# State products of batches 1 to 3 over the whole array, preparation split into single operations, last row pair by seven products, and a new order: a retention layer with an MLP mixer on one core

## The chip, the cores and the metric

The kernel runs on one core of one Trainium2 chip. The metric is device time in microseconds for one execution. Before the change three executions took 189.84 us in the median (189.46 to 190.31). A change of less than 0.5% is about what a measurement of this kernel cannot tell from none.

## The reference, cut to what matters

```python
def _attn_ref(q, k, v):                     # (4, 8, 768, 64) each
    B, H, S, D = q.shape
    gamma = 1.0 - 2.0 ** (-5.0 - np.arange(H))
    scale = 1.0 / np.sqrt(D)
    state = np.zeros((B, H, D, D))
    for t in range(S):
        state = gamma[None, :, None, None] * state + np.einsum('bhd,bhe->bhde', k[:, :, t], v[:, :, t])
        y[:, :, t] = scale * np.einsum('bhd,bhde->bhe', q[:, :, t], state)

def _moe_ref(x, w_tok1, w_tok2, w_ch1, w_ch2):   # x: (4, 768, 512), heads side by side
    xt = x.transpose(0, 2, 1)
    h = np.maximum(xt @ w_tok1, 0.0) @ w_tok2    # 768 -> 256 -> 768 over the tokens
    u = x + h.transpose(0, 2, 1)
    return u + np.maximum(u @ w_ch1, 0.0) @ w_ch2    # 512 -> 1536 -> 512 over the channels
```

## The kernel before, in words

The 768 time steps of a batch are cut into 6 chunks of 128, and the 8 heads into 4 pairs. `front(b, p)` does batch b and head pair p, 16 in all:

- K and Q are scaled by decay tables (`decayed`, L519 on ACT and L521 on DVE; tables `gk`, `gy`), and turned (`kT`, `qT`): in batch 0 on the PE (L551, L553) with an evacuation by DVE or ACT (L562, L567), in batches 1 to 3 by a DMA transpose of K and Q.
- The state of a chunk is a 64 x 64 product of K and V for each head (L582). Its 5 chunks x 2 heads are ten matmuls on quarter tiles of the array, called "wide" in the code, into one PSUM bank. Five steps on DVE then sum the states up: a copy (L592) and four multiply-adds (L594, tile `U`), each of 128 x 64 with the product read from PSUM. ACT or DVE writes them as `cross` (L605, L607).
- Scores K Q (L623, on half tiles, "high") are masked on DVE (L630, tile `am`) and multiplied by V (L641); the cross terms are added (L651). The result is `x16` (L663).
- The token mixer follows: L676, relu, L696. Its output is cast as `u16` and copied to `X`; `u16` is turned into `uT` (L732 and L738 in batch 0, a DMA in the others).

`back(b)` is the channel mixer of a batch. Batch 0 widens with plain products (L766), the others with seven half products in place of eight (`widen7`, L838, with sums on DVE, L810, kept pieces `us` on ACT or DVE, L791, and joins on DVE, L859). Then `narrow7` makes two row chunks by seven products (L962) of six matmuls of 256 columns, with four sums on DVE (L941) and five additions into `X` (L976). Only the last two chunks of batch 3 go through `narrow` (L909, added by L918): twelve matmuls of 512 columns for the one, and for the other twelve each of 256, 128 and 128 columns.

The order is written out by hand: `ORDERED` lists every operation by its number, two characters each, and `WAYS` says which of its engines does it. `arrange` goes through the list with planned costs (`act`, `dve`, the class `Rings` for the DMA queues, `FREE` for the start of each engine) and assigns buffers and PSUM banks; what is issued on each engine follows that order. Where the plan has the PE idle for over 400 ns in the first 21 us, matmuls of a zero tile into bank 7 are put in (`FILL`, L1079).

The first loads go through SP (two Q tiles called `hs` and a K tile called `us`, in float32); all others through POOL. The preparation ahead of the first products is a few operations: `away` and `since` by iota on POOL, `lgs` (L400) and the `lnh` and `gp` memsets on DVE, the `gq` tables (four Exp on ACT, L425) and `gk`, `gy` (L404, L405).

## Time and profile before

| | us |
|---|---|
| median of three executions | 189.84 |
| the profiled execution's own time | 188.9 |
| its span | 187.1 |
| PE busy | 179.3 |
| DVE busy | 168.0 |
| ACT busy | 122.5 |
| POOL busy | 52.7 |

The span runs from the first instruction of the program to its last; 1.8 us of the execution's own time lie around it. Busy time of the PE counts matmuls until their results are out, so that one overlaps the next: how far apart two matmuls start tells what each costs. The granted TensorE clock was 0.998 in the mean.

### The profile page before, as it was taken

To read this page: it belongs to the slowest core of one execution; us is meant where nothing else is said; L and a number is where in the kernel's file an instruction comes from. 1 tells how busy PE (TensorE), PEld (TensorE's weight loads), DVE (VectorE), ACT (ScalarE), POOL (GpSimd) and SP (SyncE) were. 2 spreads that over 40 slices of the span, in tenths; PEclk is the share of its full clock that TensorE was granted. 3 is DMA by queue.
4 is the path that set the end of the run, shared out by engine and by line. 5 is a ranking of instruction groups with operands and counts; after the bars stand their busy time and mean duration, and the time that the engine had idled before them with its cause. 6 is when DMAs were issued, how large, how long until landed. Compare 5 with 4: busy or idle time off the path is not lost.

```text
span 187.1 us, 5262 instructions
## 1 busy us (share of the span) xinstructions
PE 179.3 (96%) x2103; PEld 136.4 (73%) x2103; DVE 168.0 (90%) x430; ACT 122.5 (65%) x277; POOL 52.7 (28%) x61
## 2 busy tenths in 40 slices
PE   7899999999999999999999999999999999999990
PEld 2465799666788988877668889966679986668960
DVE  5479999998999999999999999998799999888871
ACT  0869789347899999999978785595754126551000
POOL 7994496562644442266004000000000000000000
PEclk9999999999999999999999999999999999999999
DMA  6999999999999999699999997242013054700062
GB/s 160 202 158 193 178 195 195 186 188 204 158 156 150 150 177 141 101 106 152 163 204 128 139 169 162 112 89 41 0 56 46 0 155 182 272 1 4 0 233 106
DMA packets 92249, 25.31 MB, mean 135 GB/s; under 512 B 81984, under 2 KB 89280, under 8 KB 92224
## 3 DMA queue, kind: packets, MB, share of 16 engines
q0 software_dynamic: 67184, 12.78, 88.1%
q1 hardware_dynamic: 23456, 9.64, 24.7%
q10 hardware_dynamic: 1584, 2.56, 3.7%
q8 instruction: 16, 0.26, 0.6%
q14 instruction: 9, 0.07, 0.1%
HBM read 26.74 MB, written 6.29 MB: 177 GB/s over the span
## 4 chain that ended last, share of the span: by engine, by line
PE 81%; DVE 10%; ACT 5%; issue 2%; POOL 1%; POOLq 0%; DVEq 0%; ACTq 0%
PE bank L962 25%; PE bank L838 18%; PE bank L766 9%; PE bank L676 6%; PE bank L696 5%; DVE am L630 3%; PE bank L909 3%; PE bank L641 3%; PE bank L623 2%; PE bank L651 2%; PE bank L582 2%; PE bank L1079 2%; PE bank L551 2%; DVE U L594 1%; ACT cross L605 1%
## 5 line engine op out<-in xcount | busy, mean ns | idle before, releaser
L791 ACT COPY us<-bank 128x384 f32<-128x384 f32 (+1 forms) x43 | 18.5, 438 | 24.4 <-PE bank L962 10.2
L630 DVE TENSOR_TENSOR am<-bank,mask 128x384 f16<-128x384 f32 x64 | 32.7, 547 | 1.0 <-PE bank L623 1.0
L786 ACT ACTIVATE h<-bank 128x384 f16<-128x384 f32 x45 | 21.5, 499 | 10.2 <-PE bank L766 7.2
L962 PEld LDWEIGHTS <-hs 128*128 128x128 f16 x264 | 24.7, 98 | 2.7
L962 PE MATMUL bank<-wsum,hs 128*128 128x256 f16 x198 | 26.4, 273 | 0.0
L482 POOL DMA_DIRECT2D v<-in_v_dram x16 | 16.7, 1042 | 34.2 <-PE bank L651 22.3
L838 PE MATMUL bank<-hs,late 128*128 128x384 f16 x108 | 23.8, 326 | 0.3 <-DVE hs L810 0.2
L859 DVE CUSTOM_DVE_ANT_0 h<-bank,us 128x384 f16<-128x384 f32 x36 | 19.1, 550 | 3.2 <-ACT us L791 1.9
L962 PEld LDWEIGHTS <-h 128*128 128x128 f16 x198 | 18.7, 98 | 2.5
L976 DVE TENSOR_TENSOR X<-X,bank 128x256 f32<-128x256 f32 x44 | 17.8, 414 | 1.5 <-PE bank L962 1.2
L838 PEld LDWEIGHTS <-late 128*128 128x128 f16 x144 | 13.3, 98 | 8.0 <-issue 0.2
L766 PE MATMUL bank<-uT,wc 128*128 128x384 f16 x96 | 17.7, 326 | 0.0
L962 PE MATMUL bank<-wc,h 128*128 128x256 f16 x132 | 17.5, 273 | 0.0
L594 DVE SCALAR_TENSOR_TENSOR U<-U,gp,bank 128x64 f32<-128x64 f32 x64 | 16.6, 274 | 0.5
L482 POOL DMA_DIRECT2D k<-in_k_dram x15 | 15.7, 1045 | 4.2 <-ACT X L663 1.7
L838 PE MATMUL bank<-uT,wc 128*128 128x384 f16 x72 | 16.3, 326 | 0.0
L605 ACT ACTIVATE cross<-U,gp 64x320 f16<-64x320 f32 x27 | 15.1, 558 | 0.7 <-DVE U L594 0.3
L696 PE MATMUL bank<-h,wt 128*128 128x128 f16 x192 | 15.0, 219 | 0.0
L663 ACT CAST x<-bank 128x384 f16<-128x384 f32 x30 | 13.9, 487 | 1.5 <-PE bank L838 0.9
L838 PEld LDWEIGHTS <-wc 128*128 128x128 f16 x108 | 10.1, 98 | 5.2
L676 PE MATMUL bank<-x,wt 128*128 128x128 f16 x192 | 13.3, 219 | 0.3 <-ACT x L663 0.2
L696 PEld LDWEIGHTS <-wt 128*128 128x128 f16 x192 | 12.2, 98 | 1.7
(87 smaller groups left out, 354.9 us busy)
## 6 DMA issues: line engine op xcount, KB each, us to landing
out_dram<-X SPq DMA_DIRECT2D x14, 256.0 KB, 2.8
v<-in_v_dram POOLq DMA_DIRECT2D x16, 192.0 KB, 7.2
k<-in_k_dram POOLq DMA_DIRECT2D x15, 192.0 KB, 7.7
q<-in_q_dram POOLq DMA_DIRECT2D x14, 192.0 KB, 8.0
wc<-in_moe_w_ch_dram POOLq DMA_DIRECT2D x5, 512.0 KB, 13.5
out_dram<-X ACTq DMA_DIRECT2D x9, 256.0 KB, 2.3
hs<-in_q_dram SPq DMA_DIRECT2D x2, 384.0 KB, 5.1
wc<-in_moe_w_ch_dram POOLq DMA_DIRECT2D x2, 256.0 KB, 8.0
```

Of the source, the lines that this page charges most:

```text
L482: (nc.sync if hard else nc.gpsimd).dma_start(out=tile_of(s, [P, 2, NC, D], FP if hard else F16), in_=src.rearrange("h (c p) d -> p (h c) d ...
L594: nc.vector.scalar_tensor_tensor(out=u[:, c], in0=u[:, c - 1], scalar=gp[:, p:p + 1], in1=st, op0=ALU.mult, op1=ALU.add)
L630: nc.vector.tensor_tensor(am, SC[g].tile[:, :m * P].rearrange("p (i t) -> p i t", t=P), mask.to_broadcast([P, m, P]), ALU.mult)
L676: nc.tensor.matmul(acc[:, jt * P:(jt + 1) * P], wt1[:, i, jt * P:(jt + 1) * P], X16.tile[:, i].rearrange("p h d -> p (h d)"), start=(i == ...
L696: nc.tensor.matmul(Y[j].tile[:, 2 * i * D:2 * (i + 1) * D], wt2[:, jt, t], H1.tile[:, jt], start=False, stop=(jt == NJ - 1), skip_group_ch ...
L766: nc.tensor.matmul(acc[:, :SH], wc1[:, ct, ft * P:(ft + 1) * P], UT.tile[:, ct, sh * SH:(sh + 1) * SH], start=(ct == 0), stop=(ct == NP - 1))
L786: nc.scalar.activation(out, src, AF.Relu)
L791: (nc.scalar.copy if e == "ACT" else nc.vector.tensor_copy)(out, src)
L838: nc.tensor.matmul(acc[:, :SH], left(ct), r[:, ct], start=first and ct == 0, stop=ct == C2 - 1, skip_group_check=True)
L859: nc.vector._custom_dve(TENSOR_ADD_SAT, out=h(m, sh), in0=R.tile[:, :SH], in1=KS.tile[:, j], s0=BIG, s1=0.0)
L962: nc.tensor.matmul(acc[:, lo], l[:, j], r[:, j], start=first and j == 0, stop=j == K2 - 1, skip_group_check=True)
L976: nc.vector.tensor_tensor(dst(), dst(), b_(), ALU.add)
```

## The change

The state products of batches 1 to 3 (`FULL`) become five matmuls of 128 x 128 in place of ten on quarter tiles: both heads' K against both heads' V. Four chunks go to one PSUM bank and the fifth to another. Of each 128 x 128 result only the two diagonal 64 x 64 blocks are states. Four copies bring them to `U` in SBUF (two of 64 x 256, two of 64 x 64; each on ACT or DVE by `WAYS`), and the four multiply-adds then work in `U` in place. The copy L592 falls away for these twelve fronts.

The preparation is cut into single operations that the order can place one by one; a tiny Exp (`warm`) stands first on ACT, so that the table load comes there. `LAST7` turns the last two chunks of batch 3 over to `narrow7`. Several dependencies on a buffer's first user are now order alone (`behind`). Planned costs change (`act`, `decayed`, `FREE`, `OPENING`, `SOFT`), and `ORDERED` and `WAYS` are new throughout.

```diff
+    OPENING = 2900
-    SOFT = 0.6
+    SOFT = 0.55
...
-FREE = dict(PE=300, ACT=2500, DVE=900, POOL=900, SP=750)
+FREE = dict(PE=300, ACT=1150, DVE=1090, POOL=1200, SP=750)
...
-    "0a090d0b0c000408030e01050j1e060h071j0f0i021f1g0g1k1h1l1i1m0l1n1P1Q1t1O1o1x1p0k1q2s1w1R1v1T1S1u0m1V1U1r2t0o23"
+    "0o0l00070q020s0p080a090g0x0h011s0v0306040b0c1x220t0d1y270r0m0i0e0u1t1u280f1v1w0w230k1H0n241K250z1I2G261L2H0y"
...
-    LAST7 = False
+    WIDE7 = {0: (), 1: range(6), 2: range(6), 3: range(6)}
+    FULL = (1, 2, 3)
+    SOURCE = ()
+    LAST7 = True
...
+    def emit():
+        nc.scalar.activation(warm, zero[:, :1], AF.Exp)
+    prep("warm", "ACT", 1350, emit)
...
-    def emit():
-        nc.scalar.activation(gk, lgs, AF.Exp, scale=-1.0)
-        nc.scalar.activation(gy, lgs, AF.Exp, bias=lnsc, scale=1.0)
-    g_op = prep("ACT", 380, emit, [lgs_op])
+    gk_op = prep("gk", "ACT", 130, lambda: nc.scalar.activation(gk, lgs, AF.Exp, scale=-1.0), [lgs_op])
+    gy_op = prep("gy", "ACT", 200, lambda: nc.scalar.activation(gy, lgs, AF.Exp, bias=lnsc, scale=1.0), [lgs_op])
...
+        gq_ops.append(prep("gq", "ACT", 605, emit, [since_op, lnh_op, lgm_op], [] if p else [GQ], [SINCE, GQ] if p else [SINCE]))
...
+    cross_ops = [prep("cross", "DVE", 330, lambda t=t: nc.vector.memset(t, 0.0)) for t in cross]
...
+        if b in FULL:
+            STs = [Slot(FA, good=2), Slot(FA)]
+
+            def emit():
+                for st in STs:
+                    tile_of(st, [P, 512], FP)
+                for c in range(NC - 1):
+                    nc.tensor.matmul(STs[c // 4].tile[:, c % 4 * P:(c % 4 + 1) * P], K.tile[:, c].rearrange("p h d -> p (h d)"),
+                                     V.tile[:, :, c], start=(c % 4 == 0), stop=True, skip_group_check=True)
+            pp = op(one("PE", (280, 440), emit), kl + [vl], STs, [K, V], key="st")
+            cp = []
+            for k in range(2):
+                for j in range(2):
+                    def emit(e, k=k, j=j):
+                        u = tile_of(US, [P, NC - 1, D], FP) if US.tile is None else US.tile
+                        n_ = 1 if k else 4
+                        copy(e, u[rows_of(j), 4 * k:4 * k + n_],
+                             STs[k].tile[rows_of(j), :n_ * P].rearrange("p (c x) -> p c x", x=P)[:, :, j * D:(j + 1) * D])
+                    cp.append(op(either(emit, ACT=act(64 if k else 256), DVE=dve(64 if k else 256)), [pp], [] if cp else [US],
+                                 ([US] if cp else []) + [STs[k]], behind=cp[0] if cp else None, key="sd"))
+            for c in range(1, NC - 1):
+                def emit(c=c):
+                    nc.vector.scalar_tensor_tensor(out=US.tile[:, c], in0=US.tile[:, c - 1], scalar=gp[:, p:p + 1],
+                                                   in1=US.tile[:, c], op0=ALU.mult, op1=ALU.add)
+                prev = op(one("DVE", (195, 280), emit), (cp[2:] if c == NC - 2 else cp[:2]) + [gp_ops[p], prev], [], [US], key="u")
```

What the new order puts where is shown at three places.

On SP, the first loads of the program, before (`hs` are the Q tiles of pairs 0 and 1, `us` is the K tile of pair 0; the turns behind them belong to later batches):

```order
L478 DMA hs_85<-in_q_dram 128x2x384
L482 DMA us_92<-in_k_dram 128x12x64
L478 DMA hs_94<-in_q_dram 128x2x384
L540 DMA_TRANSPOSE kT_1352<-k_1219 128x6x128
L540 DMA_TRANSPOSE qT_1444<-q_1430 128x6x128
```

and now:

```order
L487 DMA hs_86<-in_q_dram 128x2x384
L487 DMA hs_92<-in_q_dram 128x2x384
L491 DMA us_105<-in_k_dram 128x12x64
L549 DMA_TRANSPOSE kT_1435<-k_1353 128x6x128
L549 DMA_TRANSPOSE kT_1490<-k_1458 128x6x128
```

The K tile of pair 0 has moved from second to third. On DVE, the work just ahead of the first masked score (`am`), before:

```order
L521 TENSOR_SCALAR k_170<-us_92,gk 128x6x64
L562 TENSOR_TENSOR qT_175<-bank_151,X_125 128x768
L592 COPY U_210<-bank_197 128x64
L594 SCALAR_TENSOR_TENSOR U_210<-U_210,gp,bank_197 128x64
L521 TENSOR_SCALAR k_214<-k_101,gk 128x6x64
L594 SCALAR_TENSOR_TENSOR U_210<-U_210,gp,bank_197 128x64
L630 TENSOR_TENSOR am_239<-bank_223,mask 128x384
```

and now (`X` holds the `gq` tables; `cross`, `gp`, `lnh` and `mask` are preparation):

```order
L571 TENSOR_TENSOR qT_158<-bank_140,X_111 128x768
L449 MEMSET cross_78 128x320
L445 MEMSET gp 64x1
L446 MEMSET gp 64x1
L433 MEMSET lnh 64x1 x2
L530 TENSOR_SCALAR k_182<-us_105,gk 128x6x64
L571 TENSOR_TENSOR qT_185<-bank_160,X_111 128x768
L576 COPY kT_204<-bank_197 128x768
L448 TENSOR_SCALAR mask<-away 128x128
L449 MEMSET cross_79 128x320
L530 TENSOR_SCALAR k_208<-k_103,gk 128x6x64
L665 TENSOR_TENSOR am_232<-bank_216,mask 128x384
```

Two turned Q tiles, the evacuation of `kT` and pieces of the preparation now stand ahead of the first masked score, and the first state sums (`U`) no longer do. On ACT, the first two fronts of batch 1 now have copies of states among the relus of batch 0's channel mixer (`h`):

```order
L377 ACTIVATE h_876<-bank_897 128x384
L382 COPY U_970<-bank_949 64x256
L528 ACTIVATE k_980<-k_739,gk 128x6x64
L382 COPY U_970<-bank_950 64x64
L382 COPY U_992<-bank_973 64x256
L377 ACTIVATE h_874<-bank_926 128x384
L377 ACTIVATE h_874<-bank_988 128x384
L377 ACTIVATE h_874<-bank_983 128x384
L377 ACTIVATE h_874<-bank_967 128x384
L640 ACTIVATE cross_78<-U_970,gp 64x5x64 x2
```

Before, ACT had no such copies: the first sum of a front read the product from its bank on DVE. Of the 48 copies, 31 stand on ACT (16 of 64 x 256, 15 of 64 x 64) and 17 on DVE (8 and 9).

280 lines of the change are left out of this document (159 added, 121 removed).

## The prediction

> **What bounds the kernel now.** First the page: busy shares and the chain that ended last, by engine.
>
> ```profile
> PE 179.3 (96%) x2103; PEld 136.4 (73%) x2103; DVE 168.0 (90%) x430; ACT 122.5 (65%) x277; POOL 52.7 (28%) x61
> ...
> PE 81%; DVE 10%; ACT 5%; issue 2%; POOL 1%; POOLq 0%; DVEq 0%; ACTq 0%
> ```
>
> The PE carries four fifths of the chain. Next the windows by stage (PE, PEld, DVE, ACT, POOL busy) and the PE's waits from 26 to 154 us.
>
> ```profile
> 26.00:94.00 68.00, 67.81 (x887) 52.19 (x884) 65.75 (x162) 57.97 (x133) 31.24 (x32) 1.00 1.96 160
> 94.00:154.00 60.00, 59.77 (x698) 48.44 (x697) 57.17 (x141) 38.04 (x91) 2.03 (x2) 1.00 0.55 98
> 170.00:180.00 10.00, 10.00 (x98) 8.72 (x96) 8.45 (x21) 0.74 (x2) 0.00 (x0) 1.00 0.11 40
> ```
>
> ```profile
> PE bank L838 <- DVE hs L810: 0.2, 1, 0.2
> ```
>
> From 26 us on the PE is busy 127.58 of 128 us, and its longest wait is 0.2 us. DVE is nearly as full, 122.92 of 128, and ACT has 57.97 of 68 up to 94 us. So matmul time saved after 26 us shows in the span, as long as work added to DVE and ACT keeps inside 5.1 and 10 us of idle time. Ahead of 26 us it is otherwise: there the PE runs zero matmuls to fill gaps, and DVE sets the pace.
>
> **The opening.** DVE between 11 and 26 us, and what starts the first product:
>
> ```profile
> 11.00:26.00 15.00, 14.15 (x251) 10.90 (x250) 14.56 (x38) 11.66 (x24) 9.55 (x13) 1.00 1.81 182
> ```
>
> ```profile
> 5.60 2.50 ACT L425 ACTIVATE X<-us,lnsc,lnh 128x384 f32<-128x384 f32 x4
> 8.01 0.19 ACT L404 ACTIVATE gk<-lgs 128x8 f32<-128x8 f32 x1
> ```
>
> ```profile
> 8.23 0.42 DVE L521 TENSOR_SCALAR k<-us,gk 128x384 f16<-128x384 f32 x1 [2.07 <-ACT gk L404]
> ```
>
> ```profile
> 1.77 0.81 SPq L478 DMA_DIRECT2D hs<-in_q_dram  x1
> ```
>
> ```profile
> hs<-in_q_dram SPq DMA_DIRECT2D x1, 384.0 KB, 6.7
> ```
>
> ```profile
> 6.29 3.51 PE L1079 MATMUL bank<-zero 128*128 128x384 f16 x13
> 9.63 0.50 PE L553 MATMUL bank<-ident,k 128*128 128x128 f16 x6
> ...
> 11.02 0.51 PE L623 MATMUL bank<-qT,kT 64*128 64x128 f16 x12
> ```
>
> ```profile
> 26.14 0.65 PE L623 MATMUL bank<-qT,kT 64*128 64x128 f16 x12
> ```
>
> Before, the decay of K waits 2.07 us for `gk`, which stands behind four Exp. The change takes that wait away: `gk` now stands behind one. But the K tile is now third on SP, and the third load landed at 1.77 + 6.7 = 8.5 us, where the decay began at 8.23. So the table is no longer late, the load is, and I book no gain there. After it thirteen zero matmuls hold the PE until the turn of K at 9.63; the new order has nine at that place.
>
> I take the first score no earlier than the 11.02 of before, and count the DVE work from there to the fourth score (26.14). DVE starts its next instruction about 0.08 us before the last one's duration is over: three masks take 1.48, so one costs (1.48 - 0.55) / 2 = 0.465, by these rows.
>
> ```profile
> 12.55 1.48 DVE L630 TENSOR_TENSOR am<-bank,mask 128x384 f16<-128x384 f32 x3
> ```
>
> ```profile
> L562 DVE TENSOR_TENSOR qT<-bank,X 128x768 f16<-128x768 f16 x8 | 7.4, 947 | 0.0
> L567 DVE COPY kT<-bank 128x768 f16<-128x768 f16 x2 | 1.1, 544 | 0.0
> L607 DVE TENSOR_SCALAR cross<-U,gp 64x320 f16<-64x320 f32 x5 | 2.7, 538 | 0.1
> L594 DVE SCALAR_TENSOR_TENSOR U<-U,gp,bank 128x64 f32<-128x64 f32 x64 | 16.6, 274 | 0.5
> L592 DVE COPY U<-bank 128x64 f32<-128x64 f32 x16 | 3.3, 216 | 1.1 <-PE bank L582 0.9
> L687 DVE TENSOR_SCALAR h<-bank 128x256 f16<-128x256 f32 x1 | 0.4, 415 | 0.0
> L430 DVE MEMSET gp<- 64x1 f32 x4 | 0.2, 59 | 0.1
> ```
>
> By the new order this stretch loses one `qT` (0.87), one `kT` copy (0.46) and one `cross` (0.46), and gains two `U` steps (0.39), a `U` copy (0.14), a relu (0.33) and two memsets (0.12); the rest is the same or exchanges one 384-column copy for another. That is 1.79 - 0.98 = **0.8 us less**. Bounds: the token weights.
>
> ```profile
> 9.27 0.83 POOL L462 DMA_DIRECT2D wt<-in_moe_w_tok_dram  x1
> ```
>
> ```profile
> wt<-in_moe_w_tok_dram POOLq DMA_DIRECT2D x1, 384.0 KB, 9.5
> ```
>
> ```profile
> 20.05 0.83 PE L676 MATMUL bank<-x,wt 128*128 128x128 f16 x12 [0.16 <-DVE U L594]
> ```
>
> They are the eighth load on POOL before and after, and landed at 18.8, while the first product that uses them began at 20.05. So the opening can win 1.25 us before it meets that load, plus some of what the shorter zero run may give the first score (9.63 less 8.65, where DVE's half of K was ready, less the 0.27 by which the load is later, is 0.7): 1.5 us at most. With a K tile that lands later still, for its queue mates now go first, it can lose 0.5.
>
> **The state products.** Batches 1 to 3 have twelve fronts. A row starts where the one ahead has issued its last matmul, so differences of starts are costs.
>
> ```profile
> 71.49 0.83 PE L676 MATMUL bank<-x,wt 128*128 128x128 f16 x12
> 72.16 0.82 PE L962 MATMUL bank<-wc,hs 128*128 128x256 f16 x6
> ```
>
> ```profile
> 58.41 0.83 PE L676 MATMUL bank<-x,wt 128*128 128x128 f16 x12
> 59.17 0.35 PE L582 MATMUL bank<-v,k 128*64 128x64 f16 x10
> 59.45 0.51 PE L553 MATMUL bank<-ident,k 128*128 128x128 f16 x6
> ```
>
> ```profile
> 113.64 0.51 PE L582 MATMUL bank<-v,k 128*64 128x64 f16 x20
> 114.08 0.61 PE L962 MATMUL bank<-wc,hs 128*128 128x256 f16 x4
> ```
>
> Twelve whole-array matmuls cost 0.67, or 0.056 each; ahead of quarter tiles the same twelve cost 0.76, so entering the tiling costs 0.09. A group of ten costs 59.45 - 59.17 = 0.28, leaving included. Five whole matmuls cost 5 x 0.056 = 0.28. A group that stands alone thus gains 0.09. But three pairs of fronts already share one entry (20 in 0.44, 0.53 with entry, against 0.56 new), and three more stand beside another tiled operation, whose switch stays. That leaves three: **0.3 us less**, within 0 and 12 x 0.09 = 1.1.
>
> [...]
>
> **The copies.** Four for each front, 31 on ACT and 17 on DVE, in place of twelve L592.
>
> ```profile
> L791 ACT COPY us<-bank 128x384 f32<-128x384 f32 x26 | 12.2, 480 | 6.6 <-PE bank L838 3.9 <-DVE h L859 1.8 <-DVE am L630 0.8
> L791 ACT COPY us<-bank 128x256 f32<-128x256 f32 x17 | 6.3, 373 | 17.8 <-PE bank L962 10.2 <-DVE X L918 7.4
> L791 DVE COPY us<-bank 128x256 f32<-128x256 f32 x5 | 2.0, 417 | 0.5 <-PE bank L962 0.5
> ```
>
> No row has 64 partitions out of PSUM in this form; I take the cost of the same columns on 128. On ACT 128 columns more cost 0.107, so 64 columns cost about 0.21 in duration; less some 0.10 of overlap, 16 x 0.27 + 15 x 0.11 = 6.0 us. On DVE 8 x 0.34 + 9 x 0.14 = 4.0, less 12 x 0.14 = 1.7: 2.3 us more. What hides them is the matmul time of batches 0 to 2's channel mixers. DVE had 5.1 us idle in 128, in small pieces, so part will show: I take **0.5 us more**, near the lower end, since the PE's waits were 0.2 at a like load; ends 0 and 2.3. The multiply-adds keep their 0.19 each: only the place of one operand changes.
>
> **The last two chunks.** L909 goes, L962 comes.
>
> ```profile
> 180.17 0.82 PE L962 MATMUL bank<-wc,hs 128*128 128x256 f16 x6
> 180.83 1.89 PE L909 MATMUL bank<-wc,h 128*128 128x512 f16 x8
> ```
>
> ```profile
> 182.75 0.69 DVE L918 TENSOR_TENSOR X<-X,bank 128x512 f32<-128x512 f32 x1 [1.31 <-PE bank L909]
> ```
>
> Six of 256 columns cost 0.66, or 0.109 each; of 512 columns (1.89 - 0.38) / 7 = 0.216, with 0.38 the duration of one. Before: 12 x 0.216 + 12 x 0.109 + 24 x 0.056 = 5.24. Now 42 x 0.109 = 4.58: **0.65 us less**. The four added sums and keeps fall where DVE has 1.5 us idle in 10 and ACT nearly all; in the order the sums stand two or three products ahead of their use. The last addition has 256 columns (about 0.42, as the copy above) in place of 0.69: **0.25 less**. The last store stays one of 128 rows. Ends: 0 and 1.1 less together.
>
> **The sum.** 0.8 + 0.3 + 0.65 + 0.25 - 0.5 = 1.5 us less. The profiled execution of 188.9 (span 187.1 and 1.8 around it) would take 187.4. It lies 0.94 below the median of 189.84; against that median the time is 188.3, and I predict that. A change within 0.5% (0.95 us, 188.9 to 190.8) can hardly be told from none.
>
> **Rivals.**
> - *DVE and ACT become the bound between 26 and 150 us.* For it: DVE at 96% and ACT at 85% up to 94 us, and both get more. Against: the PE's waits of 0.2. If none of DVE's idle time can be used, 2.3 shows in place of 0.5: 190.1. Chance 0.22.
> - *Slower: the copies put ACT's queue into the chain of each front.* Before, the first sum took the product from PSUM on DVE; now it waits for ACT copies that stand behind relus and evacuations. The place is the eight fronts whose states are made from 50 to 101 us; seven have a wide copy on ACT. Price: 0.37 for the copy and 0.48 for a 384-column operation ahead of it, 7 x 0.85 = 6.0 us in place of 0.5; it decides from the point where the PE has less than 0.85 us of other matmuls between a front's state and its cross product. If half of the fronts meet it 190.8, if all 193.8. Chance of 190.8 or more: 0.14.
> - *The opening wins all it can*, 1.5 in place of 0.8, and the copies hide: 187.1. For it: the wait for `gk` and the zero run are gone; against it, DVE's count. Chance 0.14.
> - *Multiply-adds in SBUF are cheaper.* A copy of their shape costs 0.216 in place of 0.274; if reading SBUF gave each of 48 steps that 0.06, DVE would have 2.8 us less to do, all of the copies' load, and the 0.5 would go: 187.8. Against it: a copy does less than a multiply-add, and the page has no such step from SBUF alone. Chance 0.08. [...]
>
> **How the numbers follow.** The forecast (187.6 to 189.2 as its own range) has 0.42. Faster by over 0.5%: four fifths of the forecast, the won opening and the cheap steps, 0.34 + 0.14 + 0.08 = 0.56. Within 0.5%: the rest of the forecast and most of the first rival, 0.08 + 0.19 = 0.27. Slower: the ACT chain and the first rival's end, 0.14 + 0.03 = 0.17. The range takes in the won opening with hidden copies and half of the 0.8 that more lone state groups could give (187.1 - 0.4 = 186.7), and the first rival to 190.5; it leaves out the ACT chain and a few hundredths below.
>
> **What would show it.** The fourth score at 25.3 rather than 26.1; five state matmuls 0.28 after their start with no 0.09 ahead; `U` copies on ACT near 0.37 and 0.2; PE waits from 26 to 154 us of less than 1 us in sum, and a last addition of 0.42. The prediction is wrong if the PE waits for `cross` or `x` in batches 1 and 2, or if the K tile lands after 9 us.

## The result, and the profile after

The changed kernel takes 191.98 us in the median of five executions (191.41 to 192.81), the one before 189.84 (189.33 to 190.31): a ratio of 1.0115 with an interval of 1.0078 to 1.0152. It is slower by 2.1 us where 1.5 us less had been forecast. The profiled execution took 192.81 us, with a span of 191.0. Where a median below and its ratio do not go together, the ratio counts: it leaves disturbed executions out.

The page of the changed kernel, busy shares and the chain by engine:

```profile
PE 180.5 (95%) x2030; PEld 137.2 (72%) x2030; DVE 175.0 (92%) x439; ACT 132.3 (69%) x313; POOL 52.2 (27%) x61
...
PE 70%; DVE 20%; ACT 3%; issue 2%; DMA 2%; DVEq 0%; ACTq 0%
```

DVE has 7.0 us more to do (5.5 in a second pair of profiles, the runs e15 and e14 below), ACT 9.8, and DVE's share of the chain has doubled. Of DVE's 7.0 the copies are only 2.9: 5.3 for them, less 2.4 for the twelve copies L592 that are gone. The rest is work that the new `WAYS` and `LAST7` give to DVE: decays, casts, relus, half-sums. The windows by stage (PE, PEld, DVE, ACT, POOL busy):

```profile
26.00:94.00 68.00, 66.12 (x817) 50.80 (x815) 64.86 (x155) 58.16 (x140) 32.26 (x35) 1.00 1.81 149
94.00:154.00 60.00, 59.60 (x663) 46.44 (x662) 58.14 (x143) 45.00 (x112) 2.88 (x3) 1.00 0.83 124
```

The PE is idle for 1.88 us up to 94 us, where it was idle for 0.19 (busy time counts a matmul until its result is out, so a wait shows here only in part). The waits of PE from 26 to 154 us (total, times, longest):

```profile
PE bank L658 <- DVE U L382: 0.6, 2, 0.4
PE bank L658 <- ACT u L698: 0.4, 1, 0.4
PE bank L676 <- DVE U L382: 0.3, 1, 0.3
PE bank L775 <- DVE u L698: 0.2, 1, 0.2
PE bank L810 <- DVE U L382: 0.2, 1, 0.2
PE bank L1027 <- DVE X L1041: 0.2, 1, 0.2
```

The scores (L658), the products with V (L676) and batch 0's channel mixer (L810) wait for a copy of `U` (L382 with tile `U`), the new operation. The stretch with three of these waits, DVE first, then PE:

```profile
43.35 0.94 DVE L1117 TENSOR_TENSOR late<-wc 128x1536 f16<-128x1536 f16 x1
44.21 0.94 DVE L1117 TENSOR_TENSOR late<-wc,late 128x1536 f16<-128x1536 f16 x1
45.19 0.43 DVE L382 COPY U<-bank 64x256 f32<-64x256 f32 x1
45.65 0.84 DVE L530 TENSOR_SCALAR k<-k,gk 128x384 f16<-128x384 f16 x1
46.52 0.56 DVE L576 COPY kT<-bank 128x768 f16<-128x768 f16 x1
47.00 0.28 DVE L609 SCALAR_TENSOR_TENSOR U<-U,gp 128x64 f32<-128x64 f32 x1
47.30 0.43 DVE L382 COPY U<-bank 64x256 f32<-64x256 f32 x1
```

```profile
44.71 0.44 PE L594 MATMUL bank<-v,k 128*128 128x128 f16 x5
44.98 0.49 PE L810 MATMUL bank<-uT,wc 128*128 128x384 f16 x2
45.67 1.46 PE L810 MATMUL bank<-uT,wc 128*128 128x384 f16 x8 [0.20 <-DVE U L382]
47.14 0.23 PE L658 MATMUL bank<-qT,kT 64*128 64x128 f16 x1
47.79 0.34 PE L658 MATMUL bank<-qT,kT 64*128 64x128 f16 x6 [0.42 <-DVE U L382]
48.35 0.32 PE L658 MATMUL bank<-qT,kT 64*128 64x128 f16 x5 [0.22 <-DVE U L382]
```

The second state product is issued by 44.98. Its copy on DVE starts 2.3 us later, because the end of the second weight sum, another copy, a decay, the evacuation of `kT` and a multiply-add stand ahead of it. The scores need the bank that it empties, and the PE starts a single score matmul and stops.

For a bill the PE's time from the fourth score to the last product is split up. Each matmul gets its usual step (0.056 for 128 columns, 0.109 for 256, and so on), each change of tiling 0.09 to 0.11 (43 of the 45 changes after 26 us in the first profile of before add 0.09 to 0.10), and what is left are waits. The split is an estimate.

| us | before | after | difference |
|---|---|---|---|
| fourth score starts | 26.14 | 26.41 | +0.3 |
| matmul steps and changes of tiling | 156.1 | 155.2 | -0.9 |
| waits of the PE | 0.1 | 5.3 | +5.2 |
| last product to the end of the span | 4.76 | 4.01 | -0.75 |
| span | 187.1 | 191.0 | +3.9 |

The sum of the second and third line, +4.3, comes straight from the rows. How it divides hangs on what is taken as a usual step: other choices, made over all runs, give from 0.9 less to 0.4 more for the second line and 3.9 to 5.2 more for the third. Either way the waits took several times what the matmuls can have won.

These are two single executions, 0.9 us below their median and 0.8 above. A second profile of each (the runs e14 and e15) puts the waits at 4.5 us after, in an execution that took its median, and at 3.3 before, in one 1.8 us above it. An execution of the median time before would have some 1.5 us of waits, as an estimate: 189.84 less 1.8 around the span, 4.76 at the end, 156.1 of steps and 25.7 for the fourth score (the median of eight profiles with that opening). So the change costs a typical execution nearer 3 us in waits than 5.2.

### The profile page after: what moved, and what is told of

It reads as the page before. It is cut to its first block, busy times and chain, and to the rows that moved or that the text cites. A ratio compares the mean times of both kernels' runs of the same rounds, so it can differ in the third digit from the quotient of the medians.

```text
span 191.0 us, 5175 instructions
## 1 busy us (share of the span) xinstructions
PE 180.5 (95%) x2030; PEld 137.2 (72%) x2030; DVE 175.0 (92%) x439; ACT 132.3 (69%) x313; POOL 52.2 (27%) x61
## 4 chain that ended last, share of the span: by engine, by line
PE 70%; DVE 20%; ACT 3%; issue 2%; DMA 2%; DVEq 0%; ACTq 0%
PE bank L1027 26%; PE bank L897 18%; DVE am L665 5%; PE bank L712 5%; PE bank L810 5%; PE bank L732 4%; PE bank L676 3%; PE bank L658 2%; PE bank L686 2%; DVE late L1117 2%; DMA hs<-in_q_dram 2%; PE bank L1145 2%; DVE U L382 2%; DVE X L1041 1%; DVE k L530 1%
## 5 line engine op out<-in xcount | busy, mean ns | idle before, releaser
L382 ACT COPY us<-bank 128x384 f32<-128x384 f32 (+1 forms) x52 | 22.7, 436 | 19.9 <-PE bank L1027 16.4
L1027 PEld LDWEIGHTS <-hs 128*128 128x128 f16 x288 | 27.4, 98 | 3.6 <-issue 0.5
L377 ACT ACTIVATE h<-bank 128x384 f16<-128x384 f32 x48 | 22.7, 497 | 8.6 <-PE bank L810 6.6
L1027 PE MATMUL bank<-wsum,hs 128*128 128x256 f16 x216 | 28.0, 272 | 0.2 <-DVE X L1041 0.2
L1027 PEld LDWEIGHTS <-h 128*128 128x128 f16 x216 | 20.5, 98 | 3.5
L1041 DVE TENSOR_TENSOR X<-X,bank 128x256 f32<-128x256 f32 x48 | 19.0, 413 | 0.9 <-PE bank L1027 0.7
L1027 PE MATMUL bank<-wc,h 128*128 128x256 f16 x144 | 19.6, 272 | 0.0
L810 PE MATMUL bank<-uT,wc 128*128 128x384 f16 x96 | 17.2, 326 | 0.2 <-DVE U L382 0.2
L609 DVE SCALAR_TENSOR_TENSOR U<-U,gp 128x64 f32<-128x64 f32 x48 | 13.0, 276 | 1.2 <-ACT U L382 0.9
L698 ACT CAST x<-bank 128x384 f16<-128x384 f32 x28 | 12.5, 482 | 0.9 <-PE bank L686 0.6
```

What stands on the lines that cost most here:

```text
L377: nc.scalar.activation(out, src, AF.Relu)
L382: (nc.scalar.copy if e == "ACT" else nc.vector.tensor_copy)(out, src)
L810: nc.tensor.matmul(acc[:, :SH], wc1[:, ct, ft * P:(ft + 1) * P], UT.tile[:, ct, sh * SH:(sh + 1) * SH], start=(ct == 0), stop=(ct == NP - 1))
L1027: nc.tensor.matmul(acc[:, lo], l[:, j], r[:, j], start=first and j == 0, stop=j == K2 - 1, skip_group_check=True)
L1041: nc.vector.tensor_tensor(dst(), dst(), b_(), ALU.add)
```

## The experiments

Theory A: the copies cost the time, since DVE and ACT have no room for them. Theory B: the new order and its choice of engines cost it. Each ratio is to the kernel before, run beside it on the same chip. "Waits" are those of the PE after the fourth score, "busy" is from the page; both belong to the one profiled execution, whose own time stands ahead of them. Those of e1, e9 and e15 lie 2 to 3 us above their medians, so their waits are high for the run. Only seven of the eighteen medians fell into a range that was expected of the run (e6, e8, e12 to e16); the others chose a theory by the nearer end, or none.

| run | median | ratio, interval | profiled | fourth score | waits | DVE, ACT busy |
|---|---|---|---|---|---|---|
| e1 tiles, new order | 194.25 | 1.0222, 1.0171 to 1.0273 | 197.5 | 25.38 | 9.6 | 171.8, 125.2 |
| e2 copies, old order | 196.7 | 1.0357, 1.0309 to 1.0405 | 197.23 | 26.71 | 8.0 | 171.6, 130.8 |
| e3 tail, old order | 189.43 | 0.9979, 0.9942 to 1.0016 | 190.31 | 25.80 | 2.6 | 169.8, 124.8 |
| e4 late sums moved | 193.76 | 1.0218, 1.0174 to 1.0261 | 193.37 | 25.61 | 6.6 | 174.5, 132.2 |
| e5 half the copies | 187.84 | 0.9914, 0.9882 to 0.9947 | 188.21 | 25.61 | 1.4 | 169.3, 128.2 |
| e6 copies of tiles | 196.73 | 1.0395, 1.0343 to 1.0447 | 196.0 | 25.48 | 7.9 | 171.6, 131.0 |
| e7 decays on ACT | 193.85 | 1.0233, 1.0189 to 1.0277 | 194.67 | 26.18 | 7.3 | 172.2, 134.2 |
| e8 copies, batch 3 | 193.01 | 1.0194, 1.0142 to 1.0246 | 193.71 | 25.63 | 5.4 | 169.9, 125.7 |
| e9 tiles, two copies | 191.78 | 1.0056, 1.0014 to 1.0097 | 193.82 | 27.45 | 3.7 | 170.1, 128.7 |
| e10 tiles, one copy | 189.81 | 1.0005, 0.9972 to 1.0038 | 189.56 | 25.59 | 1.3 | 169.3, 128.0 |
| e11 half, on DVE | 188.34 | 0.9927, 0.9896 to 0.9959 | 188.16 | 25.60 | 1.5 | 172.0, 126.4 |
| e12 fewer zero products | 192.26 | 1.0141, 1.0088 to 1.0193 | 191.69 | 25.39 | 5.0 | 174.9, 132.2 |
| e13 copies unawaited | 191.6 | 1.0094, 1.0065 to 1.0123 | 190.25 | 25.60 | 3.4 | 172.7, 131.4 |
| e14 after, again | 191.68 | 1.0105, 1.0067 to 1.0143 | 191.61 | 25.89 | 4.5 | 174.4, 132.1 |
| e15 before, again | 189.65 | 0.9982, 0.9947 to 1.0016 | 191.47 | 25.55 | 3.3 | 168.9, 122.6 |
| e16 tail, one ACT copy | 189.04 | 0.997, 0.9941 to 0.9999 | 188.71 | 25.52 | 1.3 | 168.6, 128.6 |
| e17 dummies from SBUF | 189.93 | 0.9989, 0.9958 to 1.0019 | 189.64 | 25.60 | 2.9 | 173.8, 131.5 |
| e18 tail, copy, decays | 188.89 | 0.9936, 0.9904 to 0.9968 | 189.68 | 26.80 | 1.0 | 169.2, 127.1 |

**Copies or order: e1 and e2.** The changed kernel without the copies, and the kernel before with them.

```diff
-    FULL = (1, 2, 3)
+    FULL = ()
...
-                for c in range(NC - 1):
+                for c in range(NC if b else NC - 1):
```

> The changed kernel in its own order, but with the state products of batches 1 to 3 as quarter-tile products again: ten (plus two that only fill columns 320 to 384 of the bank) in one bank, the first step again one 128x64 copy out of the bank, the other four steps reading the bank. The 48 copies of diagonal blocks are gone; the steps of eight fronts were drawn ahead of the masked scores that stood among them, so that the bank comes free. Theory A (the copies): the 2.1 us of loss come from the copies, about 7 us of extra work on DVE and ACT and banks held until a copy comes, so the three waits of PE for them at 45.6 to 48.4 us (0.36, 0.61 and 0.40) and those at 88.4 and 95.7 (0.43 and 0.16) go: 189.3 to 190.6 us, PE waits after 26 us under 3.5 us in sum (5.3 in the changed kernel). Theory B (the order: decays on DVE beside POOL's DMA issues, late sums ahead of what PE waits for): nothing much goes, 191.5 to 192.5, and PE waits stay at 4.5 to 6 us.

```diff
-                    nc.vector.tensor_copy(u[:, 0], st)
+            for k in range(2):
+                for j in range(2):
+                    copy(e, u[rows_of(j), 4 * k:4 * k + n_], STs[k].tile[rows_of(j), ...][:, :, j * D:(j + 1) * D])
```

> The kernel before, in its old order, with the whole-array state products for batches 1 to 3 and their four copies each put where the first step's copy stood, on the engines that the changed kernel uses (31 on ACT, 17 on DVE). Nothing else changed. Theory A (the copies cost it): 191.3 to 192.5 us, PE waits after 26 us of 3 us or more (0.08 before). Theory B (the order): the switches of the quarter-tile groups saved and the copies hidden, 189.3 to 190.2, PE waits under 1 us.

Put into the old order, the copies cost 3.6%, some 7 us, with 8.0 us of waits: more than theory A gave them. Taking them out of the new order does not help either: 194.25 us, outside both ranges. The new order has its state steps elsewhere and holds the one bank until the last of them, so its scores now wait for steps (2.5 us in four waits of the profiled execution). The quarter tiles also cost the PE more for steps and changes of tiling, some 1.4 us against e5 (the changes 2.4 more, the rest 1.0 less, as counted in what was expected of e9). Neither theory stands alone. The copies cost 7 us there, and the new order, with its tail and opening, ends 5 us below e2: it suits the copies as the old one does not. e1 cannot show the price of the copies in the new order, because they also empty the banks early there, and because the products went back with them.

**The tail alone: e3.** Only the last two chunks of batch 3, with the last 74 operations in the changed kernel's order.

```diff
-    LAST7 = False
+    LAST7 = True
```

> The kernel before with only the last two chunks of batch 3 done as the others are (seven products in place of eight and the final three pieces), the end of the order (the last 74 operations) taken from the changed kernel. Both theories: the tail's terms hold, 42 x 0.109 us in place of 5.24 us and a shorter end after the last matmul (4.0 us against 4.76), 188.9 to 189.3 us. If the four half-sums that the seven products add make DVE late at the end, 189.6 to 190.3.

0.9979 with an interval of 0.9942 to 1.0016: 0.4 us less in the ratio, where 0.9 had been forecast; both no change and the forecast's 0.9 (0.9953) lie within the interval. The half-sums did not make it slower. In the profile the tail shows more clearly: by each choice of usual steps the PE's steps are 0.6 us less than before, and from the last product to the end are 4.52 us in place of 4.76.

**Local repairs: e4 and e7.** In e4 the two sums L1117 of the rows above move behind the half-sums at 62 us; in e7 four decays that DVE did slowly go to ACT.

```diff
 DVE, in order
-late sums 2 and 3
 U copy of front (1, 0)
...
 half-sum 3 of narrow7, batch 0
+late sums 2 and 3
```

> The changed kernel with the last two of the four weight sums of the late kind (0.94 us each, at 43.35 and 44.21 us on DVE, just ahead of the U copies that PE waits for) moved behind the half-sums at about 62 us; they are first read at about 84. Theory A1 (the waits at 45 to 48 us are local: copies queued behind two long instructions): the three waits of 1.4 us in sum go and do not come back, 190.3 to 191.2 us. Theory A2 (DVE is full from 40 to 140 us, and the end is set by its amount of work): they go there and as much comes back behind 62 us, 191.5 to 192.5.

```diff
-DVE: K decays (1, 1) second head, (1, 2) first head, (2, 2) second head; Q decay (2, 2) second head
+ACT: the same four, at the same places of the order
```

> The changed kernel with the four decays that took 865, 842, 509 and 912 ns on DVE beside an instruction of POOL (at 42.56, 45.65, 76.44 and 83.95 us; an undisturbed one takes 310) given to ACT, at about 0.51 us each. Theory C (decays held up by POOL's DMA issues are what makes DVE late): DVE does 3.1 us less, 190.0 to 191.2 us, and the waits at 45.67 to 48.35 us (1.4 in sum) fall under 0.5. Theory B (the order is tight on ACT as well): 191.4 to 193, with new waits for ACT.

Both are slower than the changed kernel by over 1%. In e4 two of the three waits at 45 to 48 us are gone, but the sums now run from 61.06 to 62.9, and waits of 0.93 and 0.96 stand behind them at 63.3 and 64.3 (by the view the first is for a cast on ACT, the second for DVE). In e7 DVE is busy 2.8 us less, and a new wait of 2.1 us appears. Its rows, of PE and of ACT:

```profile
83.41 0.48 PE L897 MATMUL bank<-uT,wc 128*128 128x384 f16 x2 [2.08 <-ACT bank L382]
```

```profile
82.89 0.46 ACT L382 COPY bank<-bank 128x384 f32<-128x384 f32 x1 [1.09 <-DVE am L665]
```

ACT starts the seed copy that the PE waits for only when DVE's mask has emptied a bank. A shift on one engine turned up as a wait on another. So theory C, that slowed decays make DVE late, is not borne out: without them DVE has 2.8 us less to do, and the time is longer.

**How much the copies take in the new order: e5 and e11.** Two copies a front in place of four, everything else in its place; e5 keeps those on ACT, e11 those on DVE. These kernels, and e13 and e17 below, leave out the states of each pair's second head: they tell what a copy costs and are no versions to use.

```diff
-                for j in range(2):
-                    copy(e, u[rows_of(j), 4 * k:4 * k + n_], st[rows_of(j), :, j * D:(j + 1) * D])
+                copy(e, u[:, 4 * k:4 * k + n_], st[:, :, :D])
```

> The changed kernel with two copies a front in place of four: one of 128x256 and one of 128x64, which take the first head's block for both halves of the partitions, so the lower half's states are other numbers than they should be. 24 copies are left, 22 on ACT and 2 on DVE (48 before, 31 and 17); the second bank and the steps in SBUF stay. Theory A (the work of the copies on two full engines): DVE does 15 copies less (about 4.5 us), ACT 9 (about 2.5 us), 189.5 to 190.8 us, PE waits after 26 us of 3.5 us or less. Theory B (an order this tight loses by any shift of its engines, and less work alone brings little): 191.3 to 192.5, waits 4.5 us or more.

> As the run with half the copies, with the other choice: 24 copies are left, 15 on DVE and 9 on ACT (that run: 2 and 22). DVE does 2 copies less than in the changed kernel, ACT 22 less (about 7 us). The lower half's states are other numbers again. Theory A-DVE (what costs is the copies on DVE, which is at 0.91 to 1.0 from 40 to 140 us): little comes back, 191.0 to 192.3 us. Theory A-both (either engine's queue makes PE wait, ACT's as well): 188.5 to 190.0 us.

Half of the copies away brings 187.84 and 188.34 us, below the kernel before and below the ranges expected of them (by 1.7 and 0.2), with waits of 1.4 and 1.5. It does not matter, by these intervals, whether 15 copies leave DVE and 9 ACT, or 2 leave DVE and 22 ACT. So the price is not that of the fuller engine alone, though ACT is busy for only 0.69 of the span. Order, products, banks, tail and opening are the changed kernel's here: with 24 copies in place of 48 it would have been the forecast's 188.3.

**What a copy costs by: e6, e13 and e17.** Three candidates: the second bank, a step that waits for two copies, and the engines. e6 puts the four copies behind quarter-tile products in one bank, in the old order. In e13 24 copies write to a tile that nobody reads. In e17 these 24 also read a constant in SBUF, not the bank.

```diff
-            STs = [Slot(FA, good=2), Slot(FA)]
+            ST = Slot(FA, good=1)
```

> The kernel before in its old order with its quarter-tile state products in one bank, and the four copies a front of the same sizes on the same engines as in the run with copies in the old order; the steps then go in SBUF. So the copies are there without the whole-array products and without a second bank. Theory A (the copies' work and the time a step waits for them): as slow as with the whole-array products, 195 to 197.5 us. Theory A2 (the second bank, which must be free before a product may start): under 192.5.

```diff
-            copy(e, u[rows_of(j), 4 * k:4 * k + n_], st[rows_of(j), :, j * D:(j + 1) * D])
+            copy(e, dump[e][rows_of(j), :n_], st[rows_of(j), :, j * D:(j + 1) * D])
```

> The changed kernel with all 48 copies on their engines, in their places and of their sizes' columns, but 24 of them write to a tile that nobody reads; the other 24 cover all 128 partitions, as in the run with half the copies, and the steps wait for these alone. The lower half's states are other numbers. The banks come free when all copies are done, as in the changed kernel. Theory W (the copies cost by the time they take on two engines that are nearly full, and so push back what stands behind them): 191.2 to 192.5 us, PE waits after 26 us of 4.5 us or more. Theory D (a step waits for the later of two copies, on two engines): 187.5 to 188.9 us, waits of 2 us or less.

```diff
-            copy(e, dump[e][rows_of(j), :n_], st[rows_of(j), :, j * D:(j + 1) * D])
+            if e == "ACT":
+                copy(e, o_, i_)
+            else:
+                nc.vector.tensor_tensor(o_, i_, i_, ALU.add)
```

> As the run with unawaited copies, but the 24 operations that nobody reads take their input from a constant in SBUF and not from the bank, so they wait for no product and hold no bank (on ACT a copy, on DVE an addition of the same columns). Places, engines and columns are the same; the lower half's states are other numbers. Theory W1 (time on two engines that are nearly full): 190.8 to 192.3 us, PE waits after 26 us of 3 us or more. Theory W2 (banks held until the copy's turn): 187.5 to 189.0 us, waits under 2 us.

e6 is as slow as e2, so the second bank is not it. e13 is as slow as the changed kernel, so the steps' waiting is not it. The dummies of e17 take what the copies of e13 take; first e13's groups, then e17's:

```profile
L382 DVE COPY dumpDVE<-bank 64x256 f32<-64x256 f32 x7 | 2.9, 421 | 1.3 <-ACT U L382 1.1
L382 ACT COPY dumpACT<-bank 64x256 f32<-64x256 f32 x5 | 1.8, 368 | 0.1
```

```profile
L623 DVE TENSOR_TENSOR dumpDVE<-away 64x256 f32<-64x256 f32 x7 | 2.9, 417 | 0.1
L382 ACT COPY dumpACT<-away 64x256 f32<-64x256 f32 x5 | 2.0, 403 | 0.1
```

The ratios make steps: 0.9914 with 24 copies, 0.9989 with 24 dummies more, 1.0094 when these read the bank, and 1.0105 or 1.0115 when the steps wait for them too. So of 24 copies' price about 0.75% (1.4 us) is time on the engines and 1.05% (2.0 us) comes from reading the bank. Two things come with that. The bank stays taken until the copy's turn comes (2.3 us for the DVE copy at 47.30 above). And the engine stands idle ahead of a copy until what it waits for is done: 1.3 us before the dumps on DVE in the row above, 1.1 of them put down to ACT's `U` copies, and 0.1 in e17. Where the two copies of a bank stand on different engines, the second comes after the first in the trace, and where it had to wait (0.18, 0.28 and 0.23 us at 50.30, 95.43 and 111.53 us) the view puts that down to the first, so that one queue's delay passes to the other. The last of the three in the changed kernel, DVE and then ACT:

```profile
111.26 0.23 DVE L382 COPY U<-bank 64x64 f32<-64x64 f32 x1
```

```profile
111.53 0.20 ACT L382 COPY U<-bank 64x64 f32<-64x64 f32 x1 [0.23 <-DVE U L382]
```

In e13 such waits come to 1.3 us on DVE and 0.9 on ACT. e5, e11 and e17 have one reader a bank and do without them. No run here divides the 2.0 us between these waits and the held bank. The intervals of e5, e17 and e13 do not touch, the first two by little; each ratio was taken on another chip beside the kernel before, and e17 ended between the ranges of its two theories. The last, at 0.1 to 0.2%, is nothing that these runs can tell. The order on each engine is the same in e13 and e17; which bank a product gets is the planner's choice and may differ.

**Is it a price for each front: e8.** Whole-array products and copies in batch 3 alone, old order.

```diff
+    FULL = (3,)
```

> The kernel before in its old order with whole-array state products and their copies for batch 3 alone (four fronts of twelve). Theory A with a price for each front that is the same in every batch: a third of the 7.0 us that all twelve cost, 191.6 to 192.6 us. If the price sits where DVE and ACT are fullest (batches 1 and 2, 45 to 100 us): under 190.8. If it sits at the two long waits for a copy on ACT (1.37 and 1.20 us at 107.5 and 121.3 us): 192.6 to 194.

1.9% for a third of the fronts, over half of what all cost: it looks like a price for places, not for each front. The place, ACT and then PE:

```profile
102.84 0.48 ACT L693 CAST u<-bank 128x384 f16<-128x384 f32 x1 [0.25 <-PE bank L726]
103.21 2.19 ACT L372 COPY U<-bank 64x256 f32<-64x256 f32 x7
```

```profile
104.01 0.83 PE L706 MATMUL bank<-x,wt 128*128 128x128 f16 x12 [1.21 <-ACT U L372]
```

Copies of two fronts stand in one row on ACT (the view joins seven, named by the first), behind a cast of 128x384; the next token product wants a bank that they hold (by the view's releaser). That one wait and its like at 117.84 us (1.04) are 2.2 of the 3.7 us. This profile also has waits of 0.97 and 0.7 us, at 73 and 95 us, that are not put down to copies of `U`.

**Whole array or tiles: e9 and e10.** The changed order with quarter-tile products in one bank, two copies or one copy a front over all partitions, with all states.

```diff
-                         STs[k].tile[rows_of(j), :n_ * P].rearrange("p (c x) -> p c x", x=P)[:, :, j * D:(j + 1) * D])
+                    copy(e, u[:, lo_:lo_ + n_], ST.tile[:, lo_ * D:(lo_ + n_) * D].rearrange("p (c x) -> p c x", x=D))
```

> The changed kernel with quarter-tile state products in one bank (two more a group, which only fill columns 320 to 384) and two copies a front over all 128 partitions, 128x256 and 128x64, 22 on ACT and 2 on DVE where the run with half the copies has them. All states are right. Theory A (the copies' work): half the copies' gain stays, less what the products give back: PE's switches rise by about 2.4 us and its work falls by about 1.0 (the run with tiles in the new order against the one with half the copies), so 187.84 + 1.4 = 189.2 us, 188.4 to 190.0. Theory B (the second bank and the whole-array products are what the new order needs): 192 or more.

> As the run with tiles and two copies, but one copy a front, 128x320, on ACT where the first one stood (12 copies in all; an estimate from 0.37 us for 64x256 and 0.2 for 64x64: 0.42 us each). ACT does about 2 us less; the first step waits 0.06 us longer for its copy. Theory A: 0 to 0.6 us below that run, 188.0 to 189.5 us. Theory B: the same as that run within 0.4 us, since ACT is not what PE waits for.

e10 (11 of its copies on ACT, one on DVE) gives 1.0005: the waits are as low as in e5, 1.3, and what separates the two is the PE's own bill, 1.6 us more for steps and changes of tiling. Two products a group only fill columns there, 24 in all or some 0.5 us, an estimate from 20 such products in 0.44; so the whole-array products are worth some 1.1 us in an order built for them. e9, with twice the copies, came to 1.0056. Its 191.78 us lie between its two ranges, and e10's 189.81 above its own.

**The opening: e12.** Half of the zero products.

```diff
-    FILL, F_NS = 0.7, 165
+    FILL, F_NS = 0.35, 165
```

> The changed kernel with half as many zero products in the opening (the factor 0.7 is 0.35). Theory O1 (the zero run of nine, 7.33 to 10.03 us, stands in the way of the K turn, whose K was ready at about 9.1): K turn 0.6 to 0.9 us earlier, fourth score 0.3 to 0.9 us earlier, 191.1 to 191.7 us. Theory O2 (the opening hangs on the loads, the first token weight landing at 18.1 us, and a lower granted clock takes back the rest): fourth score within 0.2 us, 191.8 to 192.6 us.

The PE in its opening and at the fourth score:

```profile
7.67 1.46 PE L1145 MATMUL bank<-zero 128*128 128x384 f16 x4
8.92 0.85 PE L562 MATMUL bank<-ident,k 128*128 128x128 f16 x6
...
25.39 0.60 PE L658 MATMUL bank<-qT,kT 64*128 64x128 f16 x12
```

The turn of K comes at 8.92 in place of 10.03 and the fourth score 0.5 us ahead of the second profile of the changed kernel. But of the nine runs in the table that have the changed kernel's opening, operation by operation and with all the zero products, seven have a fourth score at 25.38 to 25.61 too. The median is 192.26, as O2 expected: fewer zero products bring nothing that can be seen.

**Both kernels again: e14 and e15.** No edit.

> The changed kernel once more, for a second profile and beside the others on one chip. If the slow zero run and K turn of the opening (granted clock 7 and 8 tenths in the second and third slice) were that one execution's, the fourth score stands near 25.4 us in place of 26.41 and the span is about 1 us shorter, with PE waits after 26 us of 5.0 to 5.4 us again; 191.4 to 192.4 us.

> The kernel before once more, for a second profile. Its first profile was of an execution 0.9 us below its median. If a typical execution has waits that the first one lacked, PE waits after 26 us are 0.5 to 2 us here (0.08 there), and the difference between the two kernels' waits is 3.3 to 4.8 us and not 5.2; time 189.4 to 190.3 us.

In e14 the fourth score is 0.5 us earlier than in the first profile, not the 1 us expected: half of that was the one execution's. e15 shows waits that the first profile of before had lacked. Its PE, then its ACT (`ACTq` is ACT issuing a DMA):

```profile
94.86 0.51 PE L623 MATMUL bank<-qT,kT 64*128 64x128 f16 x12 [0.96 <-DMA qT<-q]
...
101.80 0.38 PE L676 MATMUL bank<-x,wt 128*128 128x128 f16 x4 [2.09 <-ACT x L663]
```

```profile
97.33 3.90 ACTq L895 DMA_DIRECT2D out_dram<-X  x1
...
101.27 0.48 ACT L663 CAST x<-bank 128x384 f16<-128x384 f32 x1 [2.79 <-issue]
```

A turned Q tile landed late. The longer wait has another reason: the cast that the token product needs stood on ACT behind a store whose issue held the queue for 3.90 us. The same store took 1.97 us to issue in the first profile of before, 3.79 in e3 (with a wait of 1.98 at the same product), and 0.38 in e16 and e18. Why it varies is not shown. The ten executions of e15 run from 187.92 to 192.14, the six of e14 from 191.61 to 192.66: the kernel before is not free of waits, and how many it has changes from one execution to the next.

**One copy a front in the old order: e16 and e18.** The old order with the new tail, quarter-tile products in one bank, and one 128x320 copy a front on ACT in place of the first step's copy on DVE. e18 also gives four decays to DVE.

```diff
-                    nc.vector.tensor_copy(u[:, 0], st)
+                copy(e, u, ST.tile[:, :(NC - 1) * D].rearrange("p (c x) -> p c x", x=D))
```

> The kernel before with the last two chunks of batch 3 in seven products, as in the run with the tail in the old order, and in batches 1 to 3 one copy of 128x320 on ACT in place of the first step's 128x64 copy on DVE, from a quarter-tile product in one bank; the steps go in SBUF. Correct states. If copies cost by work on the fuller engine: DVE does 2.7 us less (12 x 0.23), ACT some 5 us more (12 x 0.42, an estimate from the copies of 64x256 and 64x64), ACT is at 0.65: 188.4 to 189.6 us, below both kernels. If what costs is whatever ACT's queue holds behind a copy that waits for its product: 190.5 to 193 us.

```diff
-ACT: K decays (2, 1) second head, (2, 2) second head, (2, 3) first head, (3, 0) first head
+DVE: the same four, at the same places of the order
```

> The kernel with the new tail and one copy a front on ACT, with four decays of batches 2 and 3 (ACT 0.62 us each, between 69 and 84 us) given to DVE, where they take 0.31 undisturbed and where 0.9 to 1.4 us in ten are idle in that stretch. If the waits for ACT's copies at 72 and 85 us (0.62 and 0.44) are ACT's load: 188.0 to 188.8 us. If an order this tight loses by any exchange, as the run with decays on ACT did: 189.3 to 191.

e16 is faster than the kernel before by 0.3% (0.01 to 0.59), e18 by 0.6% (0.3 to 1.0), at 188.89 us; against the changed kernel, by way of the kernel before, that is 0.9936 / 1.0105 = 0.983. e16's interval barely leaves out no change, and e16 and e18 cannot be told apart from each other. Part of the gain is the tail's (0.2% in e3), and both profiles have the short issue of the store above; what the copy alone brings is not separated. One copy that relieves the fuller engine costs nothing to speak of, where four cost 7 us.

## Why the prediction was wrong, point by point

- **What bounds the kernel.** That matmul time saved shows in the span held for the tail, in e3's profile. "As long as work added to DVE and ACT keeps inside 5.1 and 10 us of idle time" is the step that failed. DVE and ACT kept idle time in the changed kernel (3.1 and 9.8 of 68 us up to 94 us), and the PE waited for them: half of the copies cost 3.4 us. Idle time in small pieces is no room: an added operation goes to a place in a queue, and what stands behind it is late. The sum also put at nothing what the new `WAYS` and `LAST7` add to DVE beside the copies, 4.1 us of its 7.0 (2.6 of 5.5 in the second pair). And "the PE's waits were 0.2 at a like load" was read from one execution, 0.9 us below the median, while e15, 1.8 above it, has 3.3 us of waits with the same order.
- **The copies.** This is the term that was wrong: 0.5 us, ends 0 and 2.3. The durations were right (0.37 and 0.21 on ACT forecast, 371 and 206 ns measured):

```profile
L382 ACT COPY U<-bank 64x256 f32<-64x256 f32 x16 | 5.9, 371 | 0.2
L382 DVE COPY U<-bank 64x256 f32<-64x256 f32 x8 | 3.3, 418 | 0.1
L382 ACT COPY U<-bank 64x64 f32<-64x64 f32 x15 | 3.1, 206 | 0.6 <-DVE U L382 0.4
L382 DVE COPY U<-bank 64x64 f32<-64x64 f32 x9 | 2.0, 222 | 0.5 <-ACT U L382 0.3
L609 DVE SCALAR_TENSOR_TENSOR U<-U,gp 128x64 f32<-128x64 f32 x48 | 13.0, 276 | 1.2 <-ACT U L382 0.9
```

  The upper end was DVE's added work alone. Half of the copies cost 3.4 us in the new order (1.0094 less 0.9914, of 189.7) and all of them 7 in the old, through both engines and through banks. The upper end could have come from the rival's price, 0.85 for a copy and the operation ahead of it, for all twelve fronts: 10.2.
- **The rival of DVE and ACT as the bound** had the mechanism but a price of 2.3, DVE's work alone. **The rival of ACT's queue** had the size, 190.8 to 193.8, but put the wait into the steps. Its sign, a PE that waits for `cross` or `x`, is not among the six waits above, and in e13 it costs nothing to speak of that the steps wait for half of the copies only. It is the bank behind the copy that the next product wants (the waits for `U` L382, and e8's row). That 191.98 lies in this rival's span is in part luck.
- **The state products**, 0.3 less: the price of a group was right, five take 0.27 (44.71 to 44.98 in the rows above). The sum is smaller than the bill can tell: 0.9 less for steps and switches, less the tail's 0.65, leaves 0.25, and other choices of the usual step leave nothing. e10 against e5 shows some 1.1, but in an order built for whole-array products. Ten on quarter tiles took 0.28 before (59.17 to 59.45), so the two kinds of group cost the same but for the way into the tiling, 0.09 where a group stands alone.
- **The opening**, 0.8 less: wrong. In both pairs of profiles the fourth score came 0.3 us later, but that is the executions' chance: eight profiles have the old opening and eleven the new one (e12 apart), and their fourth scores are at 25.7 and 25.6 us in the median. From the first score to the fourth DVE's stretch is 0.2 to 0.3 shorter in both pairs (15.12 to 14.89 in the first), not 0.8. The DVE rows of that stretch have two more decays (21.26 and 22.00 us), a memset of `cross` (11.61) and a copy to `X` (25.12) that the count does not name, 1.2 us by their steps, and DVE is busy for 14.47 of the 15 us from 11 to 26 us, where it was for 14.56. The K tile ended ACT's wait at 8.50, as forecast:

```profile
8.50 0.61 ACT L528 ACTIVATE k<-us,gk 128x384 f16<-128x384 f32 x1 [1.64 <-DMA us<-in_k_dram]
```

  The zero products hold up the turn of K only in some executions. In the first profile after, nine took 0.30 us each, with a granted clock of 7 and 8 tenths in its second and third slice, and the turn came at 10.03; before, thirteen took 3.51. In e15 (before) and e4 (the changed kernel's opening) they were done in time, and the turn waits for the decay on ACT:

```profile
5.96 2.29 PE L1079 MATMUL bank<-zero 128*128 128x384 f16 x13
8.95 0.51 PE L553 MATMUL bank<-ident,k 128*128 128x128 f16 x6 [0.70 <-ACT k L519]
```

```profile
6.73 1.64 PE L1145 MATMUL bank<-zero 128*128 128x384 f16 x9
9.18 0.49 PE L562 MATMUL bank<-ident,k 128*128 128x128 f16 x6 [0.82 <-ACT k L528]
```

  So 11.02, where the forecast began to count, was itself one execution's: the first score is at 10.35 in e15 and 10.41 in e4.
- **The last two chunks**, 0.65 and 0.25 less: e3's profile bears them out (0.6 in steps, 0.24 behind the last product), and the last addition takes 0.42. By time e3 shows 0.4 with an interval that holds no change too.
- **Cheaper multiply-adds in SBUF**: the 0.06 us less a step does not show. A step takes 276 ns in `U` alone (L609 above) against 274 with the product in PSUM; its other input was in SBUF before too.

## What to carry to other kernels

Where two engines beside the bound are nearly full, as here (DVE and ACT idle for 3.1 and 9.8 of 68 us, and half of the copies cost 3.4), an added operation is priced by its place: what it waits for at the head of its queue, what stands behind it, and which bank or buffer it keeps until its turn comes; the idle time summed over a stage says little. Before a profile's waits or its opening are taken as a kernel's, look at where its execution lies among the timed ones, and take a second. An order that was fitted to its operations belongs to them: judge such a change by putting its operation into the old order and by thinning it out in the new one. A single move in such an order can cost (1.0218 and 1.0233 in e4 and e7, against 1.0115) or cost nothing (0.9936 in e18, against 0.997 in e16).

## What the runs showed of the hardware

Decays in f16 from SBUF take 310 ns on DVE, but some take 509 to 912 while POOL issues a DMA (42.56, 45.65, 76.44 and 83.95 us in the first profile after; one is in the rows above at 45.65). In every one of them a POOL instruction of 1.01 to 1.05 us covers most of it, but not every covered decay is slow: one at 41.41 took 307. In the second profile (e14) three are slow, and the counterpart of 45.65 takes 321 with POOL issuing a DMA all the while; what decides between the two is not shown. The multiply-adds in `U` take 265 to 286 ns throughout (first profile after). By e7, giving the slow ones to ACT wins nothing.

The issue of one and the same store on ACT's queue held ACT for 0.38 to 3.90 us (e16 and e15), and the PE behind it for 2.09. Two copies out of one PSUM bank by two engines went one after the other in the first profile after: at 50, 95 and 111 us the second began 0.03 to 0.04 us after the first had ended, released by it as the view infers. What they would do without that wait no run shows.
